# Moving two unit loads from ScalarE's to SyncE's queue, and turning the rows of three early jobs on VectorE instead of TensorE

## The chip, the cores and the metric

The kernel runs on one core of one Trainium2 chip. Its time is the time of one execution on the device, in microseconds (us); three runs were made of the kernel before, and one further execution was profiled. The profile names the engines PE (TensorE, matrix products and 128x128 transposes), PEld (TensorE's weight loads), DVE (VectorE), ACT (ScalarE), POOL (GpSimd) and SP (SyncE, which only issues DMAs). ACT, POOL and SP each have a queue of their own from which they issue DMAs; the profile writes ACTq, POOLq, SPq for it.

## The reference

The input is a sequence batch `x` of 4 x 3648 tokens of 256 channels, and a gate logit of the same shape. First comes a gated scan along each sequence, then a mixture of 16 experts in 4 groups (each token goes to one expert):

```python
f = lower_bound + (1 - lower_bound) * sigmoid(f_logit); i = 1 - f
for t in range(S): h = f[:, t] * h + i[:, t] * x[:, t]; y[:, t] = h      # 4 x 3648 x 256
x = y.reshape(14592, 256)
g_idx = argmax(x @ w_group); g_w = softmax weight of that group
e_idx = argmax(x[group g] @ w_expert[g]); e_w = softmax weight of that expert
out[token] = g_w * e_w * (relu(x[token] @ w1[g, e]) @ w2[g, e])          # 256 -> 1024 -> 256
```

## The kernel before, in words

The tokens are cut into 29 **units** of 512. A unit's input is one tile `zt` of 1 MB (gate logits and x, transposed: channels on partitions), loaded by `p1_load`. There are four `zt` buffers, so the load of unit u must wait until unit u-4 is through with its buffer. `ZX_SP = 9` decides which engine issues the load: units below 9 from SP's queue, the others from ACT's, where the issuing instruction stands in ACT's own order between its computations. Then ACT takes the tanh (L188) and an affine map (L198), DVE makes the gated input (L214, L234) and the scan `h` (L225), PE transposes `h` back to rows (L252), which ACT copies out as `rows` (L254, L256), and PE makes the router's scores (L266, L277; ACT copies them at L269 and L278 as `rs` and `Lg`). A chain of small DVE operations (L287 to L343, or to L382 in the first units) turns the scores of one or two units into a position `posi` for each token. POOL scatters the rows, 128 at a time, into lists by expert in a DRAM buffer `xs` (L347, an indirect DMA). A row of `xs` is 258 words: 256 channels, the token's number and its weight.

The experts' products are done in 32 **jobs** and a remainder. The first 16, the early jobs, one for each expert, run while the scan still goes on: `EARLY` gives for each a unit (the cut) and a number of 128-row tiles; the job takes so many rows of that expert's list as soon as the rows of all units before the cut are scattered. The early jobs 12 and 13 have 640 rows, 14 and 15 have 768. Then come 16 late jobs "B" with what is left in each list. A job loads its weights in 512 KB pieces `st` (L809), which ACT splits to a high part `wh` (L817) and DVE to a low part `wl` (L818); loads its rows (`job_rows`); brings them into the transposed form by `job_xt`; and multiplies in `m1_step` (L914 to L916, three products of high and low parts, then a relu `hh` on ACT at L919 and its low part `hl` on DVE at L920) and `m2_step` (L944). Loads, splits and transposes of a job are issued while the job before it multiplies; the rows of jobs 13 and 14 are asked for by `early_rows`, those of job 15 by `start_macro`, which runs after the last routing is issued.

In `job_rows` an early job loads each piece of up to 256 rows by one DMA (L791): partition p takes whole rows, 1032 bytes each. In `job_xt` PE then transposes each 128x128 block into a PSUM tile `ps_p` (L861), ACT casts it to `xh` (L870), DVE makes the low part `xl` (L871) and copies the tokens' numbers and weights to `meta` (L873). A job B does without PE: its rows come by four **quarter** loads (L767), each of which brings 64 of the 256 channels of all rows to 32 partitions in runs of 256 bytes, and DVE turns the 32x32 blocks in place (L848).

Each engine runs its instructions in an order that is fixed when the kernel is built: in the first part of the scan as the code issues them, later as a scheduler places them by its own estimate of when their operands come. DMAs of SP and ACT signal their ends on eight counters, DMAHW0 to DMAHW7, which the DMAs of both queues take in turn in the program's order; a DMA that takes a counter waits for the counter's last user to have landed. POOL's scatters use counters named DMASW. `early_loads` and `scatters` hold the row loads and the scatters already issued; `declare_no_dep` says of a pair that the one need not wait for the other.

Of the kernel before, what the change touches and what calls it, by code (L numbers as in the profile page):

```python
# [10 lines left out]
F32 = mybir.dt.float32  # L11
F16 = mybir.dt.float16
BF16 = mybir.dt.bfloat16
I32 = mybir.dt.int32
AF = mybir.ActivationFunctionType
ALU = mybir.AluOpType
AX = mybir.AxisListType.X

P = 128
# [18 lines left out]
X_BUFS = 4  # L38
AHEAD = 3
MT = -(-max(CAPS) // 128)  # L40
ZX_SP = 9


@with_exitstack
def gated_scan_moe(ctx: ExitStack, tc, zx, lower, wroute, wexp, out, S):
    nc = tc.nc
    sync = nc.sync
    ctx.enter_context(nc.allow_low_precision(reason="whole numbers small enough to be exact"))
    N, D = out.shape
    KD = D // P  # L50
# [9 lines left out]
    xs = nc.dram_tensor("xs", [LROWS, RW], I32).ap()  # L60
# [7 lines left out]
    mo = ctx.enter_context(tc.tile_pool(name="mo", bufs=2))  # L68
# [5 lines left out]
    def bank(tag):  # L74
        return ps.tile([P, UNIT], F32, name=f"ps_{tag}", tag=tag, bufs=PS_BUFS[tag])
# [79 lines left out]
    at = 0  # L155
# [7 lines left out]
    def p1_load(u):  # L163
# [13 lines left out]
        else:  # L177
            last_load[u] = (nc.sync if u < ZX_SP else nc.scalar).dma_start(out=zt[:, :, :, 0:w], in_=src[:, :, :, 0:w])
        units[u] = {"z": zt}
# [397 lines left out]
    def early_rows(u):  # L577
        asked.add(-u)
        for mac in macros:
            for j in mac:  # L580
                if j.kind == "A" and EARLY[j.idx][0] == u and j.idx < NE - 1:
                    job_rows(j)

    regs = {}
    early_loads = []
# [164 lines left out]
    def job_rows(j):  # L750
        e = job_e(j)
        queue = sync
        if j.kind == "A":
            pos = queue.value_load(j.pos[0:1, e:e + 1], min_val=e * LW + PRE - j.len, max_val=e * LW + PRE + N)
        elif j.kind == "B":
            pos = sync.value_load(regs["pordi"][0:1, j.idx:j.idx + 1], min_val=0,
                                  max_val=(NE - 1) * LW + PRE + N)
        else:
            pos = sync.value_load(regs["tabs"][0:1, 3 * j.idx + 1:3 * j.idx + 2], min_val=0, max_val=LIST)
        if j.kind != "A":  # L760
            job_mask(j)
        j.rows, j.meta = [], []
        if j.kind == "B":
            j.blocks = -(-j.len // 32)
            j.xb = p1.tile([P, 2, KD, UNIT], F32, name="zt", bufs=4).rearrange("p a b c -> p (a b c)")
            for q in range(P // 32):
                sync.dma_start(  # L767
                    out=j.xb.bitcast(I32)[32 * q:32 * q + 32, 0:j.blocks * KD * 32].rearrange("p (i c) -> p i c", c=KD * 32),
                    in_=xs[bass.ds(pos, j.blocks * 32), q * KD * 32:(q + 1) * KD * 32].rearrange("(i p) c -> p i c", p=32))
            j.info = mo.tile([P, MT + 1, 2], I32, name="info", bufs=6)  # L770
            full = [p for ps_ in j.parts for p in ps_ if p[2] == 1]
            nf, j.tails = len(full), [p for ps_ in j.parts for p in ps_ if p[2] > 1]
            sync.dma_start(out=j.info[:, 0:nf],
                           in_=xs[bass.ds(pos, nf * P), D:D + 2].rearrange("(t p) c -> p t c", p=P))
            for i, (b, _, g) in enumerate(j.tails):
                src = xs[bass.ds(pos + b, P // g), D:D + 2]
                for h in range(g):
                    sync.dma_start(out=j.info[h * (P // g):(h + 1) * (P // g), nf + i], in_=src)
            return
        for b, n in j.pieces:  # L780
            r = mo.tile([P, 2, RW], I32, name="xr", bufs=XR_BUFS)
            w = P if j.kind == "A" and j.tiles == 2 else n
            for q in range(0, n, w):
                at = pos + b + q
                if j.kind == "A" and b + q + w < j.len:

                    low = e * LW + PRE - (P if j.tiles == 2 else 2 * P)
                    above = at - low
                    at = ((above >= 0) * above + low).with_bounds(min_val=low, max_val=e * LW + PRE + N)
                m = w // P  # L790
                ld = queue.dma_start(out=r[:, q // P:q // P + m],  # L791
                                     in_=xs[bass.ds(at, w), :].rearrange("(p k) c -> p k c", k=m))
                if j.kind == "A":
                    early_loads.append(ld.ins)
                for u, sc in scatters:
                    if u >= EARLY[j.idx][0]:
                        tc.declare_no_dep(ld.ins, sc, reason="rows scattered behind a cut lie above it")
            j.rows.append(r)
# [21 lines left out]
    def job_xt(j, pi):  # L820
        b0, rows = j.pieces[pi]
        ch = max(i for i, (a, _) in enumerate(j.chunks) if a <= b0)
        c0 = b0 - j.chunks[ch][0]
        if j.raw:
            j.xh[ch] = mo.tile([P, 2 * P], F32, name="xh", bufs=X_BUFS)
            j.xl[ch] = mo.tile([P, 2 * P], F32, name="xl", bufs=X_BUFS)
        elif c0 == 0:
            j.xh[ch] = mo.tile([P, KD, 2 * P], F16, name="xh", bufs=X_BUFS)
            j.xl[ch] = mo.tile([P, KD, 2 * P], BF16, name="xl", bufs=X_BUFS)
        if j.kind == "B":  # L830
            if pi == 0:
                j.xt = p1.tile([P, 2, KD, UNIT], F32, name="zt", bufs=4).rearrange("p a b c -> p (a b c)")
                j.done = 0
                nf = j.tiles if not j.tails else j.tails[0][0] // P
                if nf:
                    nc.vector.copy_predicated(out=j.info[:, 0:nf, 0], mask=j.mask[:, 0:nf], data=nowhere[:, 0:nf])
                for i, (b, _, g) in enumerate(j.tails):
                    dest = mo.tile([P, 1], F32, name="dest", bufs=4)
                    nc.vector.tensor_scalar(out=dest, in0=rowmod[g], scalar1=regs["nclip"][:, j.idx:j.idx + 1],
                                            scalar2=-float(b), op0=ALU.subtract, op1=ALU.is_ge)  # L840
                    nc.vector.tensor_scalar(out=dest, in0=dest, scalar1=float(g * N), scalar2=part[g],
                                            op0=ALU.mult, op1=ALU.add)
                    col = j.info[:, nf + i, 0:1]
                    nc.vector.scalar_tensor_tensor(out=col, in0=col, scalar=float(g), in1=dest,
                                                   op0=ALU.mult, op1=ALU.add)
            upto = min(j.blocks, -(-(b0 + rows) // 32))
            xt = j.xt[:, 0:KD * j.blocks * 32].rearrange("p (k i r) -> p i k r", k=KD, r=32)
            nc.vector.transpose(out=xt[:, j.done:upto],  # L848
                                in_=j.xb[:, j.done * KD * 32:upto * KD * 32].rearrange("p (i c k) -> p i k c", k=KD, c=32))
            j.done = upto  # L850
            src = j.xt[:, 0:KD * j.blocks * 32].rearrange("p (k x) -> p k x", k=KD)[:, :, b0:b0 + rows]
            hi = j.xh[ch][:, :, c0:c0 + rows]
            nc.scalar.copy(hi, src)
            nc.vector.tensor_tensor(out=j.xl[ch][:, :, c0:c0 + rows], in0=src, in1=hi, op=ALU.subtract)
            return
        m = rows // P
        r = j.rows[pi]
        tp = bank("p")
        for k in range(KD):
            for t in range(m):  # L860
                nc.tensor.transpose(out=tp[:, (k * m + t) * P:(k * m + t + 1) * P],  # L861
                                    in_=r.bitcast(F32)[:, t, 0:D].rearrange("p (q k) -> p k q", k=KD)[:, k],
                                    identity=ident)
        tpv = tp[:, 0:KD * rows].rearrange("p (k w) -> p k w", k=KD)
        if j.raw:
            for k, t in enumerate((j.xh[ch], j.xl[ch])):
                nc.scalar.copy(t[:, 0:rows], tpv[:, k])
        else:
            hi = j.xh[ch][:, :, c0:c0 + rows]
            nc.scalar.copy(hi, tpv)  # L870
            nc.vector.tensor_tensor(out=j.xl[ch][:, :, c0:c0 + rows], in0=tpv, in1=hi, op=ALU.subtract)  # L871
        meta = mo.tile([P, 2, 2], I32, name="meta", bufs=16)
        tc.keep_in_program_order(nc.vector.tensor_copy(meta[:, 0:m], r[:, 0:m, D:D + 2]))  # L873
        if j.kind != "A":
            nc.vector.copy_predicated(out=meta[:, 0:m, 0], mask=j.mask[:, 0:m], data=nowhere[:, 0:m])
        j.meta.append(meta)
# [173 lines left out]
    at = 0  # L1050
# [67 lines left out]
    with tc.For_i(0, left, 1) as it:  # L1118
# [4 lines left out]
        j = make_job("X", 0)  # L1123
# [54 lines left out]
```

## Time and profile before

| what | us |
|---|---|
| three runs | 787.17, 792.07, 791.59 (median 791.59) |
| the profiled execution | 788.64 |
| its span from first to last instruction | 786.9 |
| PE busy | 717.1 (91% of the span) |
| DVE busy | 531.0 (67%) |
| ACT busy | 458.2 (58%) |
| POOL busy | 289.7 (37%) |

A row of a timeline has the start (us from the span's start), the busy time, the engine, the line, the operation with its tile names as out<-in, the shape and the count; the bracket holds the idle time ahead of it and what ended it. A row with SPq or ACTq is the issuing of a DMA. The windows give for each stretch the busy time of each engine, then the TensorE clock that was granted (1.00 is full speed), the mean busy share of the 16 DMA engines and what they moved.

### The profile page before, as it was taken

The numbers are of one execution on the slowest core, as the hardware profiler recorded it, in microseconds if no ns is written. First come the engines' busy times: TensorE is split into PE (matmuls) and PEld (weight loads), VectorE is DVE, ScalarE is ACT, GpSimd is POOL, SyncE is SP. The second block draws the span as 40 slices with busy tenths as digits, with TensorE's granted clock in tenths as the row PEclk, the third lists the DMA queues.
The fourth block names the chain that finished last, engine by engine and source line by source line (L and its number), as shares of the span: only waits on it lengthen the run. The fifth ranks groups of instructions, "written<-read, shape, count | busy, mean of one in ns | idle before, by whom it ended". The sixth has DMA issues, their size and how long they took to land.

```text
span 786.9 us, 20828 instructions
## 1 busy us (share of the span) xinstructions
PE 717.1 (91%) x8089; PEld 635.1 (81%) x8089; DVE 531.0 (67%) x1046; ACT 458.2 (58%) x822; POOL 289.7 (37%) x272
## 2 busy tenths in 40 slices
PE   2653896998999999999999999999999999999995
PEld 1432785777988888889988898999999999899995
DVE  6886699698999987585744646546554676556640
ACT  6674787676887956445444545444455465455541
POOL 3662328357456643642122212223232222222232
PEclk9855898999999999999999999999999999999998
DMA  7999898999988856377455443553554455555300
GB/s 271 345 347 298 267 291 262 318 284 276 331 320 287 286 169 196 121 248 183 131 132 108 130 105 112 140 124 111 139 161 111 147 165 169 166 141 175 98 30 24
DMA packets 93733, 151.75 MB, mean 193 GB/s; under 512 B 52481, under 2 KB 62623, under 8 KB 90304
## 3 DMA queue, kind: packets, MB, share of 16 engines
q1 hardware_dynamic: 78656, 99.90, 43.9%
q0 software_dynamic: 11424, 30.02, 10.7%
q10 hardware_dynamic: 3552, 20.48, 7.5%
q8 instruction: 64, 1.05, 0.6%
q14 instruction: 37, 0.30, 0.1%
HBM read 112.69 MB, written 38.19 MB: 192 GB/s over the span
## 4 chain that ended last, share of the span: by engine, by line
PE 63%; issue 11%; DVE 10%; DMA 9%; POOL 4%; ACT 2%; SPq 0%; POOLq 0%; DVEq 0%; ACTq 0%
PE ps_m L944 28%; PE ps_m L914 7%; PE ps_m L915 7%; PE ps_m L916 7%; DMA zt<-in_zx_dram 4%; DVE wl L818 3%; POOL out_dram L957 3%; PE ps_p L914 3%; PE ps_p L916 3%; PE ps_p L915 3%; DMA xr<-xs 2%; DVE h L225 2%; DVE hl L920 2%; PE ps_p L252 2%; DMA xs<-rows,posi 1%
## 5 line engine op out<-in xcount | busy, mean ns | idle before, releaser
L944 PE MATMUL ps_m<-wl,hh 128*128 128x256 bf16 (+4 forms) x1304 | 261.2, 251 | 1.7 <-issue 1.7
L944 PE MATMUL ps_m<-wh,hl 128*128 128x256 f16 (+4 forms) x1304 | 261.4, 251 | 0.0
L944 PE MATMUL ps_m<-wh,hh 128*128 128x256 f16 (+4 forms) x1304 | 261.0, 251 | 0.0
L944 PEld LDWEIGHTS <-hh 128*128 128x128 f16 (+2 forms) x2608 | 192.3, 99 | 25.0 <-issue 5.5
L914 PE MATMUL ps_m<-xh,wh 128*128 128x256 f16 (+11 forms) x766 | 191.7, 260 | 6.8 <-DVE hl L920 6.8
L915 PE MATMUL ps_m<-xl,wh 128*128 128x256 bf16 (+11 forms) x766 | 191.6, 260 | 0.3 <-DVE xl L871 0.3
L916 PE MATMUL ps_m<-xh,wl 128*128 128x256 f16 (+11 forms) x766 | 191.6, 259 | 0.0
L818 DVE TENSOR_TENSOR wl<-st,wh 128x1024 bf16<-128x1024 f32 x124 | 149.8, 1220 | 53.8 <-ACT wh L817 53.6
L347 POOL DMA_INDIRECT xs<-rows,posi x114 | 135.2, 1186 | 132.4 <-DVE rows L329 44.9
L957 POOL DMA_INDIRECT out_dram<-o,info x75 | 87.0, 1160 | 243.5 <-ACT o L956 226.7
L920 DVE SCALAR_TENSOR_TENSOR hl<-ps_m,hh 128x512 bf16<-128x512 f32 (+9 forms) x172 | 114.8, 670 | 78.5 <-ACT hh L919 78.0
L919 ACT ACTIVATE hh<-ps_m 128x512 f16<-128x512 f32 (+9 forms) x172 | 101.1, 588 | 66.3 <-PE ps_m L916 64.6
L817 ACT CAST wh<-st 128x1024 f16<-128x1024 f32 x124 | 128.1, 1047 | 16.6 <-PE ps_m L944 8.7
L915 PEld LDWEIGHTS <-wh 128*128 128x128 f16 x1072 | 105.0, 98 | 13.2 <-issue 5.7
L914 PEld LDWEIGHTS <-wh 128*128 128x128 f16 x1072 | 105.2, 98 | 10.0 <-issue 2.0
L916 PEld LDWEIGHTS <-wl 128*128 128x128 bf16 x1072 | 105.0, 98 | 8.0 <-issue 0.5
L944 PEld LDWEIGHTS <-hl 128*128 128x128 bf16 (+4 forms) x1304 | 102.9, 99 | 10.1 <-issue 0.2
L957 POOL DMA_INDIRECT out_dram<-o,meta x55 | 63.1, 1147 | 114.1 <-ACT o L956 103.3
L956 ACT ACTIVATE o<-ps_m,info 128x256 f32<-128x256 f32 (+4 forms) x75 | 33.0, 441 | 85.9 <-PE ps_m L944 78.4
L914 PE MATMUL ps_p<-xh,wh 128*128 128x256 f16 (+13 forms) x306 | 73.3, 252 | 0.0
L916 PE MATMUL ps_p<-xh,wl 128*128 128x256 f16 (+13 forms) x306 | 73.3, 252 | 0.0
L915 PE MATMUL ps_p<-xl,wh 128*128 128x256 bf16 (+13 forms) x306 | 73.3, 252 | 0.0
(165 smaller groups left out, 772.8 us busy)
## 6 DMA issues: line engine op xcount, KB each, us to landing
st<-in_wexp_dram SPq DMA_DIRECT2D x124, 512.0 KB, 6.6
zt<-in_zx_dram ACTq DMA_DIRECT2D x19, 1024.0 KB, 8.7
zt<-in_zx_dram SPq DMA_DIRECT2D x7, 1024.0 KB
xs<-blank SPq DMA_DIRECT2D x26, 258.0 KB, 4.3
xr<-xs SPq DMA_DIRECT2D x19, 258.0 KB, 5.2
xr<-xs SPq DMA_DIRECT2D x17, 129.0 KB, 2.4
xs<-rows,posi POOLq DMA_INDIRECT x114, 7.1
zt<-xs SPq DMA_DIRECT2D x8, 152.0 KB
```

The source lines that it names most:

```text
L225: nc.vector.tensor_tensor_scan(out=h[:, k, c0 - a:c1 - a], data0=ff[:, k, c0 - a:c1 - a], data1=uu[:, k, c0 - a:c1 - a], initial=init, op0 ...
L347: sc = nc.gpsimd.indirect_dma_start(out=xs_v[G["t0"] + t][:, :], out_offset=bass.IndirectOffsetOnAxis(ap=R["posi"][:, t:t + 1], axis=0), i ...
L817: nc.scalar.copy(j.wh[i], j.st[i])
L818: nc.vector.tensor_tensor(out=j.wl[i], in0=j.st[i], in1=j.wh[i], op=ALU.subtract)
L914: nc.tensor.matmul(po, w1_at(j.wh, k, c), xh[:, k], start=(k == 0), stop=False)
L915: nc.tensor.matmul(po, w1_at(j.wh, k, c), xl[:, k], start=False, stop=False)
L916: nc.tensor.matmul(po, w1_at(j.wl, k, c), xh[:, k], start=False, stop=(k == KD - 1))
L919: nc.scalar.activation(hi, pv, AF.Relu)
L920: nc.vector.scalar_tensor_tensor(out=j.hl[ch][:, cs[0]:cs[-1] + 1, 0:w], in0=pv, scalar=0.0, in1=hi, op0=ALU.max, op1=ALU.subtract)
L944: nc.tensor.matmul(pm[i * q:i * q + n, 0:dw], h[ch][:, c, ts], w2_at(w, c)[:, i * dw:(i + 1) * dw], start=(c == 0 and s == 0), stop=(c == ...
L956: nc.scalar.activation(o[s, 0:dw], pm[s, 0:dw], AF.Copy, scale=lt.bitcast(F32)[s, r, 1:2])
L957: nc.gpsimd.indirect_dma_start(out=out_v[out_n[0]].rearrange("n (g d) -> (n g) d", g=g), out_offset=bass.IndirectOffsetOnAxis(ap=lt[s, r, ...
```

## The change

`ZX_SP` becomes 11: the loads of units 9 and 10 (the tenth and eleventh) are issued by SP. And for the early jobs in `QUARTERS = (13, 14, 15)` each piece of rows is loaded as four quarters and a small DMA for numbers and weights; DVE turns the blocks from there into the PSUM tile, and PE's transposes and the copies of `meta` fall away.

```diff
-ZX_SP = 9
+QUARTERS = (13, 14, 15)
+ZX_SP = 11
...
                 m = w // P
+                if j.kind == "A" and e in QUARTERS:
+                    flat = r.rearrange("p a c -> p (a c)")
+                    for s in range(P // 32):
+                        ld = queue.dma_start(
+                            out=flat[32 * s:32 * s + 32, 0:KD * w].rearrange("p (i c) -> p i c", c=KD * 32),
+                            in_=xs[bass.ds(at, w), s * KD * 32:(s + 1) * KD * 32].rearrange("(i p) c -> p i c", p=32))
+                        early_loads.append(ld.ins)
+                    meta = mo.tile([P, 2, 2], I32, name="meta", bufs=16)
+                    ld = queue.dma_start(out=meta[:, 0:m],
+                                         in_=xs[bass.ds(at, w), D:D + 2].rearrange("(t p) c -> p t c", p=P))
+                    early_loads.append(ld.ins)
+                    j.meta.append(meta)
+                    continue
...
+        if j.kind == "A" and j.idx in QUARTERS:
+            tp = bank("p")
+            tpv = tp[:, 0:KD * rows].rearrange("p (k w) -> p k w", k=KD)
+            src = r.bitcast(F32).rearrange("p a c -> p (a c)")[:, 0:KD * rows]
+            nc.vector.transpose(out=tp[:, 0:KD * rows].rearrange("p (k i r) -> p i k r", k=KD, r=32),
+                                in_=src.rearrange("p (i c k) -> p i k c", k=KD, c=32))
+            hi = j.xh[ch][:, :, c0:c0 + rows]
+            nc.scalar.copy(hi, tpv)
+            nc.vector.tensor_tensor(out=j.xl[ch][:, :, c0:c0 + rows], in0=tpv, in1=hi, op=ALU.subtract)
+            return
         tp = bank("p")
```

The new path returns ahead of the loop that calls `declare_no_dep`, so these loads wait for every scatter that was issued before them. Each of the three jobs has three pieces: 256, 128, 256 rows in job 13 and 256 three times in 14 and 15. So 9 row loads become 36 quarter loads and 9 loads of `meta`; 10 + 12 + 12 = 34 transposes on PE become 9 on DVE; 9 copies of `meta` on DVE fall away.

Most lines behind the first insertion shift: L178 becomes L179, L188 L189, L278 L279, L559 L560, L791 L805, L809 L823, L818 L832, L871 L880 in the new path, L920 L944. New are L795 (a quarter load), L800 (the load of `meta`), L876 (the transpose on DVE) and L879 (the cast behind it).

**The order of ACT around the loads of units 11 and 12.** Here `rows` are the row copies, `rs` and `Lg` the router's copies, and L188 is the tanh of unit 9. Before:

```order
L254 COPY rows<-ps_p 128x2x256 [waits PE_49]
L178 DMA zt<-in_zx_dram 128x2048 [waits DMAHW2_49,DVE_49]
L269 COPY rs<-ps_p 128x128 [waits PE_49]
L178 DMA zt<-in_zx_dram 128x2048 [waits DMAHW5_49,DVE_49]
L278 COPY Lg<-ps_p 128x80 [waits PE_49]
L188 ACTIVATE zt<-zt 128x1024 [waits DMAHW3_49]
```

And in the changed kernel:

```order
L255 COPY rows<-ps_p 128x2x256 [waits PE_49]
L179 DMA zt<-in_zx_dram 128x2048 [waits DVE_49]
L270 COPY rs<-ps_p 128x128 [waits PE_49]
L179 DMA zt<-in_zx_dram 128x2048 [waits DMAHW3_49,DVE_49]
L279 COPY Lg<-ps_p 128x80 [waits PE_49]
L189 ACTIVATE zt<-zt 128x1024 [waits DMAHW2_49]
```

What moved: the second load, that of unit 12, waited for counter DMAHW5 and now waits for DMAHW3; its place among ACT's work is the same. The tanh behind it is in both that of unit 10, which waits for that unit's own load.

**The order of SP ahead of the first early rows**, which shows who uses these counters. `st` are weights, `blank` fills of the lists, `posA` the first early positions, `xr` the first early rows. Before:

```order
L809 DMA st<-in_wexp_dram 128x1024 [waits DMAHW7_49]
L559 DMA xs<-blank 128x258 [waits DMAHW0_49]
L559 DMA xs<-blank 128x258 [waits DMAHW1_49]
L559 DMA xs<-blank 256x1x258 [waits DMAHW2_49]
L754 TENSOR_LOAD posA [waits DVE_49]
L791 DMA xr<-xs 128x258 [waits DMASW5_49,DMASW4_49,DMASW6_49,DMASW3_49,DMASW7_49,DMASW2_49,DMAHW4_49,DMASW1_49,DMASW0_49]
L791 DMA xr<-xs 128x258 [waits DMAHW5_49]
```

And in the changed kernel:

```order
L823 DMA st<-in_wexp_dram 128x1024 [waits DMAHW6_49]
L179 DMA zt<-in_zx_dram 128x2048 [waits DMAHW7_49,DVE_49,Activation_49]
L560 DMA xs<-blank 128x258 [waits DMAHW0_49]
L560 DMA xs<-blank 128x258 [waits DMAHW1_49]
L179 DMA zt<-in_zx_dram 128x2048 [waits DMAHW2_49,DVE_49,Activation_49]
L560 DMA xs<-blank 256x1x258 [waits DMAHW3_49]
L755 TENSOR_LOAD posA [waits DVE_49]
```

What moved: the loads of units 9 and 10 stand ahead of the first and the third blank. Counter DMAHW5 is that of the second half of the first early rows (the last row of before); DMAHW3 is that of the last blank (the sixth row of the changed kernel).

**The order of DVE while job 12 multiplies and job 13 is prepared**, around the first transpose of job 14 in the changed kernel. `hl` is the low part of job 12's hidden layer, for which PE waits; `rest`, `key`, `h`, `rank` and so on belong to the one-time ordering of the lists. Before:

```order
L343 TENSOR_REDUCE posi<-sc 128x6
L612 TENSOR_TENSOR h<-key 128x256
L871 TENSOR_TENSOR xl<-ps_p,xh 128x512
L873 COPY meta<-xr 128x4
L319 TENSOR_REDUCE sm<-ex 128x30
L920 SCALAR_TENSOR_TENSOR hl<-ps_m_5124,hh 128x4x128
L321 SCALAR_TENSOR_TENSOR se<-sm,oh 128x24
```

And in the changed kernel:

```order
L880 TENSOR_TENSOR xl<-ps_p,xh 128x512
L344 TENSOR_REDUCE posi<-sc 128x6
L320 TENSOR_REDUCE sm<-ex 128x30
L944 SCALAR_TENSOR_TENSOR hl<-ps_m_5141,hh 128x4x128
L322 SCALAR_TENSOR_TENSOR se<-sm,oh 128x24
L601 SCALAR_TENSOR_TENSOR key<-rest,keyc 128x16
L876 STREAM_TRANSPOSE ps_p<-xr 128x8x2x32
L325 TENSOR_REDUCE s_5135<-se 128x6
```

What moved: the copy of `meta` is gone, and a transpose that waits for a quarter load stands between one `hl` and the next.

## Rows read from the trace of the kernel before

**Rows 1.** Page, part 1: busy us, share of the span, instructions.

```profile
PE 717.1 (91%) x8089; PEld 635.1 (81%) x8089; DVE 531.0 (67%) x1046; ACT 458.2 (58%) x822; POOL 289.7 (37%) x272
```

**Rows 2.** Windows by stage: start:end, length, the engines' busy time, clock, DMA share, GB/s.

```profile
60.00:85.00 25.00, 10.98 (x71) 7.85 (x72) 15.54 (x28) 11.60 (x25) 8.69 (x10) 0.57 0.92 309
...
120.00:190.00 70.00, 56.34 (x555) 47.22 (x553) 62.44 (x113) 51.03 (x95) 43.03 (x32) 0.95 0.89 281
190.00:290.00 100.00, 98.46 (x1029) 87.22 (x1027) 95.05 (x179) 78.22 (x146) 55.37 (x48) 1.00 0.86 289
290.00:390.00 100.00, 99.65 (x968) 89.70 (x966) 64.94 (x170) 50.77 (x89) 39.73 (x39) 1.00 0.58 175
```

**Rows 3.** ACT's timeline around the loads of units 11 and 12.

```profile
64.21 0.33 ACTq L178 DMA_DIRECT2D zt<-in_zx_dram  x1
65.16 0.27 ACT L269 COPY rs<-ps_p 128x128 f32<-128x128 f32 x1 [0.42 <-PE ps_p L266]
70.84 0.33 ACTq L178 DMA_DIRECT2D zt<-in_zx_dram  x1
71.22 0.23 ACT L278 COPY Lg<-ps_p 128x80 f32<-128x80 f32 x1 [5.79 <-DMA xr<-xs]
...
79.56 1.06 ACT L188 ACTIVATE zt<-zt 128x1024 f32<-128x1024 f32 x1 [4.57 <-DMA zt<-in_zx_dram]
```

**Rows 4.** Chain of waits of 59 to 92 us: start, length, what.

```profile
67.91 2.86 DMA xr<-xs
...
70.84 8.69 DMA zt<-in_zx_dram
...
81.14 1.13 PE ps_p L861 x4
```

**Rows 5.** The page's DMA issues: KB of one, median us from issue to landing.

```profile
xr<-xs SPq DMA_DIRECT2D x19, 258.0 KB, 5.2
```

**Rows 6.** Windows of 5 and 10 us, same columns as group 2.

```profile
75.00:80.00 5.00, 1.16 (x6) 0.75 (x4) 2.27 (x6) 0.44 (x1) 1.65 (x2) 0.50 1.00 414
...
330.00:340.00 10.00, 10.00 (x108) 9.15 (x105) 9.61 (x45) 3.69 (x9) 4.05 (x5) 1.00 0.42 134
...
360.00:370.00 10.00, 10.00 (x97) 8.99 (x95) 3.38 (x7) 3.67 (x7) 1.94 (x2) 1.00 0.94 159
```

**Rows 7.** Chain of waits of 300 to 395 us, job 14's first piece.

```profile
353.56 0.48 PE ps_p L861 x4
```

**Rows 8.** Instructions by line and form: count, busy us, mean ns, idle before.

```profile
L861 PE MATMUL ps_p<-ident,xr 128*128 128x128 f32 x110 | 19.3, 296 | 12.5 <-DMA xr<-xs 7.5 <-ACT rows L254 5.0
L871 DVE TENSOR_TENSOR xl<-ps_p,xh 128x512 bf16<-128x512 f32 x24 | 16.5, 685 | 8.9 <-ACT xh L870 8.8
...
L848 DVE STREAM_TRANSPOSE zt<-zt 128x512 f32<-128x512 f32 x18 | 12.5, 701 | 0.0
...
L873 DVE COPY meta<-xr 128x4 int32<-128x4 int32 x25 | 4.7, 187 | 0.0
```

**Rows 9.** DVE's timeline late in the scan.

```profile
334.37 0.68 DVE L920 SCALAR_TENSOR_TENSOR hl<-ps_m,hh 128x512 bf16<-128x512 f32 x1
...
340.89 0.68 DVE L920 SCALAR_TENSOR_TENSOR hl<-ps_m,hh 128x512 bf16<-128x512 f32 x1
...
379.96 0.70 DVE L848 STREAM_TRANSPOSE zt<-zt 128x512 f32<-128x512 f32 x1
```

**Rows 10.** SP's queue: row loads of jobs 14, 15, first job B.

```profile
329.95 1.69 SPq L791 DMA_DIRECT2D xr<-xs  x3
...
344.50 1.66 SPq L791 DMA_DIRECT2D xr<-xs  x3
...
359.04 3.94 SPq L767 DMA_DIRECT2D zt<-xs  x4
```

**Rows 11.** All 64 quarter loads of line 767.

```profile
DMA to landing us min/median/max: 1.7/3.5/7.7
```

**Rows 12.** POOL's timeline: the last scatter.

```profile
343.17 0.97 POOL L347 DMA_INDIRECT xs<-rows,posi  x1 [0.30 <-issue]
```

## The prediction

> **What bounds the kernel now.** I read the engines' totals first, then the windows by stage, then the chain of waits and the timelines of ACT, SP and DVE at the two places that the change touches.
>
> PE is busy for 717.1 us [rows 1], so a gain must take work from PE or shorten its idle time. The windows say where that is [rows 2]. From 60 to 85 us PE works 10.98 us of 25; from 120 to 190 it lacks 13.66 us; from 190 to 390 it is full (98.46 and 99.65 of 100). The reader is to see that in the first stretch no compute engine is full, while the DMA engines are at 0.92, and that from 190 to 290 DVE stands at 95.05.
>
> ACT's timeline tells why the first stretch is empty [rows 3]. At 65.16 ACT copies `rs`; then it is idle for 5.79 us, until the load of unit 12 has left its queue at 70.84, put down to "DMA xr<-xs". In the order this load waits for DMAHW5, the counter of the second half of the first early rows, and those wait for scatters. The router's copy `Lg` stands behind it (71.22), and DVE's routing, POOL's scatters and PE's transposes behind that. The chain of waits goes the same way [rows 4]: the rows' load 67.91 to 70.77, unit 12's load 70.84 to 79.53, ACT, PE at 81.14. ACT also waits 4.57 us ahead of unit 12's tanh at 79.56 [rows 3].
>
> **The change, part by part.**
>
> *Loads of units 9 and 10 to SP.* Two issues of 0.33 us each (the length of the one at 64.21 [rows 3]) leave ACT and enter SP. What counts is the counters: unit 12's load now waits for a blank, which SP issues ahead of the first early rows and which waits for no scatter. So it goes out right behind the copy at 65.16, which takes 0.27: at about 65.4 instead of 70.84, 5.4 us earlier. The first early rows stay behind their scatters; only loads of the scan come forward. On SP the two loads stand ahead of blanks; unit 10's waits for the buffer of unit 6, and the rows behind are not wanted before their scatters have landed, at 67.91 [rows 4], so I cost that at nothing. If that cover went, each us by which SP reaches the first rows later than 67.91 would cost one.
>
> The bounds of the gain: below nothing, if the transfers then meet in the stretch where the DMA engines are at 1.00 with 414 GB/s (75 to 80 us [rows 6]) and the rows of the early jobs land later; I allow 1.5 us for that, about the 8% that the engines lack to be full in 25 us, 2.0, less a part. Above, PE's transpose at 81.14 needs those rows, and 67.91 [rows 4] plus the median 5.2 us of such a load [rows 5] is 73.1: at most 8.0 us. I take **-4.5**: nearest to the 5.4 of the issue, less 0.9 because units 10, 11 and 12 now share the engines and the 8.69 us of unit 12's load [rows 4] grow. I take it to last to the end, since PE's later gaps (120 to 190) come from the same loop of scan, scatter and rows, which starts earlier as a whole. That is the weakest step.
>
> The Trainium skill, "Trainium Kernel Development and Optimization", Key Constraints, says that DMAs of the SP, ACT and POOL queues run on the same 16 engines, so issuing from several "only saves the sequencer's issue time". By that rule alone this part would be worth nothing and the sum 786.5; the trace's 5.79 us is a wait of the issuer for a completion, of which the rule does not speak.
>
> *Transposes of jobs 13 to 15.* 34 transposes leave PE. Four take 0.48 us in the chain [rows 7], 0.12 each (the mean of 296 ns by form [rows 8] counts overlapped time twice). PE is full there (99.65 of 100 [rows 2]), so 34 x 0.12 = **-4.1**. Bounds: 0 if PE waits for as much instead; -4.1 above.
>
> *On DVE.* Nine transposes come, eight of 128x512 and one of half that: the trace has them with an SBUF target at 701 ns [rows 8]. A PSUM target is not shown; `xl`, which reads PSUM, takes 685 ns for the same shape, so I take 0.70. That is at most 9 x 0.70 = 6.3 us, against nine copies at 0.187 = 1.7 us saved. DVE has 35 us to spare from 290 to 390 [rows 2], but not from 330 to 340: 9.61 of 10 [rows 6]. There job 14's first transpose now stands behind the `hl` of 334.37 and ahead of that of 340.89 [rows 9], with the ordering of the lists between; PE's products of job 12 use this `hl`. The copy that falls away gives 0.19 back, the transpose takes 0.70.
>
> *On the queues.* Each of the three jobs has 15 DMAs where it had 3. An issue costs 1.69/3 = 0.56 us at 329.95 and 3.94/4 = 0.99 at 359.04 [rows 10], so SP is held for 12 x 0.56 to 12 x 0.99, 7 to 12 us more per job. Job 14's first four quarters go out by 332.2 to 333.9; the median landing of a quarter is 3.5 us [rows 11], so they are there at 335.7 to 337.4, and the transpose is due near 335.1, behind the `hl` of 334.37 with its 0.68. That is a wait of 0.6 to 2.3 at a place with about as much loose work ahead of the next `hl`. Job 15's loads now wait for the last scatter, issued at 343.17 [rows 12], and so for its landing, a few us behind their 344.50 of now [rows 10]; they are turned from about 362 on, which covers this, and the weights behind them on SP. The first job B asks for its rows at 359.04 and turns them at 379.96 [rows 9, 10]: 21 us, less 7.7 for the slowest landing [rows 11], cover the delay on SP. If this cover went, DVE would stand still there too, with each next `hl` behind it. For DVE and queues together I take **+1.0** (0 to 6.3, the transposes' whole time; beyond that is a rival).
>
> The Trainium skill, "DMA: Bandwidth & Descriptors", Specifications, gives 512 bytes as the least transfer for line rate. The quarters' runs are 256 bytes. The trace agrees: while the first job B's quarters load, the engines are busy 0.94 for 159 GB/s, against 0.86 for 289 GB/s from 190 to 290 [rows 2, 6]. No term of the sum comes from this rule, but it is what stands behind the slower rival.
>
> **Sum:** -4.5 - 4.1 + 1.0 = -7.6 on the profiled execution's 788.64: 781.0. This execution lies 2.95 under the median of the three runs (791.59), between their ends 787.17 and 792.07, whose middle is 789.6. So I add 1.0: **782.0**.
>
> **The rivals.**
>
> *Early gain swallowed.* The part ahead of 85 us ends sooner, but from 85 to 290 the loop of loads, scan and scatters is held by DMA engines at 0.86 to 0.89 and by DVE at 95.05 of 100 [rows 2], and PE's gaps between 120 and 190 grow by what was won. For it: DVE's load there. Against it: DVE lacks 7.6 us of 70 from 120 to 190, and its own waits ahead of 85 go too. With half a us kept for the sum: -0.5 - 4.1 + 1.0 + 1.0 gives **786.0**.
>
> *More is won.* Unit 12's load comes so early that its 4.57 us wait goes as well, up to the bound of 8.0, and DVE's waits cost nothing new: 788.64 - 8.0 - 4.1 + 1.0 = **777.5**. Against it: DMA engines nearly full in that stretch.
>
> *Quarter loads late: slower.* DVE runs in order. When a quarter lands after its transpose's turn, the `hl` behind it and PE's `m2` products wait. Place: job 14's first piece near 335 and the pieces that follow, where the transposes stand well ahead of the place of PE's (353.56 [rows 7]); then job 15's and the first job B's rows, as 256-byte runs fill the engines. Price: up to the slowest landing, 7.7 us [rows 11], for each piece that is late. From 8.6 us of such waits on (4.5 + 4.1) the change is a loss; two late pieces of 7.7 on top of the sum, with the early gain swallowed, give 786.0 + 15.4 = **801.4**. Against it: of the nine pieces only job 14's are wanted within a few us of their issue.
>
> *It doesn't do what it says.* If unit 12's load were held by something else (its buffer, of unit 8), the early part would stay. That is the first rival's time.
>
> **Chances.** Forecast 0.50, with a range of its own of 779 to 785; early gain swallowed 0.28; more won 0.11; quarters late 0.11. About 1% is what a measurement of this kernel can tell from no change: below 783.7 it is faster by it, above 799.5 slower. The forecast's case lies four fifths below 783.7 (0.40), more won wholly (0.11), swallowed hardly (0.02): faster 0.53. Quarters late gives slower 0.09, the rest stays within 1%: 0.38. Range: 776 to 790, from below more won to beyond swallowed; it leaves out most of the slower rival and little at the lower end.
>
> **What would show it.** ACT's copy `Lg` at about 65.5 with no wait of 5.8 us, unit 12's tanh before 76, PE's first transposes of early rows at 76 to 77: step one. PE's idle time from 120 to 190 at 13.7 as before: it lasts; near 18: swallowed. No PE transposes from 320 on and PE still at 99% or more there: step two. DVE's transposes with waits of under 2 us put down to DMA: step three; waits of 5 and more with `hl` late: the slower rival. The prediction is wrong if the idle time of PE ahead of 85 us stays as it is, or if PE is idle for more than 3 us between 330 and 390.

## The result, and the profile after

| | before | changed |
|---|---|---|
| median of six runs, us | 789.45 (787.17 to 792.07) | 776.62 (775.32 to 780.02) |
| profiled execution, us | 788.64 | 776.59 |
| its span, us | 786.9 | 774.8 |

The ratio of the times is 0.9842, with a 95% interval of 0.9811 to 0.9873: about 12.5 us less. Forecast were 782.0 us and a range of 776 to 790; the time lies in it, 0.6 us above its lower end, but below the range of the forecast's own case (779 to 785). The windows by stage, with the columns of [rows 2]:

```profile
60.00:85.00 25.00, 19.09 (x114) 14.23 (x114) 17.99 (x30) 15.09 (x32) 10.99 (x11) 0.61 0.90 336
...
120.00:190.00 70.00, 59.66 (x574) 50.24 (x576) 59.27 (x110) 49.10 (x90) 39.70 (x34) 0.93 0.88 285
190.00:290.00 100.00, 98.45 (x1030) 87.34 (x1022) 93.97 (x177) 77.62 (x146) 56.84 (x47) 1.00 0.81 275
290.00:390.00 100.00, 99.24 (x967) 88.66 (x966) 66.67 (x157) 51.66 (x91) 37.45 (x36) 1.00 0.69 177
```

From 60 to 85 us PE works 19.09 us where it worked 10.98 [rows 2], with the DMA engines as busy as before (0.90 against 0.92), but moving more (336 against 309 GB/s). From 120 to 190 it lacks 10.3 us instead of 13.7: what was won ahead is not given back there. From 290 to 390 PE is at 99.24, a little less full than before. ACT's timeline around the loads of units 11 and 12, the part that answers [rows 3]:

```profile
64.59 0.27 ACT L270 COPY rs<-ps_p 128x128 f32<-128x128 f32 x1 [0.50 <-PE ps_p L267]
64.65 0.33 ACTq L179 DMA_DIRECT2D zt<-in_zx_dram  x1
65.42 0.23 ACT L279 COPY Lg<-ps_p 128x80 f32<-128x80 f32 x1 [0.56 <-PE ps_p L278]
...
69.34 1.06 ACT L189 ACTIVATE zt<-zt 128x1024 f32<-128x1024 f32 x1 [0.67 <-DMA zt<-in_zx_dram]
72.00 1.06 ACT L189 ACTIVATE zt<-zt 128x1024 f32<-128x1024 f32 x1 [1.61 <-DMA zt<-in_zx_dram]
```

Of the two tanhs shown, the first is unit 11's and the second unit 12's (the tanh in the two order listings of ACT is unit 10's). Unit 12's load leaves ACT's queue at 64.65, right beside the copy `rs`, and `Lg` follows at 65.42 with a wait of 0.56 us for PE, and none for a DMA. The tanh of unit 12 waits 1.61 us for its data instead of 4.57. The chain of waits of the same stretch:

```profile
63.81 0.84 DVE zt L235
64.65 7.33 DMA zt<-in_zx_dram
...
73.59 1.13 PE ps_p L885 x4
```

The load takes 7.33 us where it took 8.69 [rows 4], and PE's first transposes of early rows stand at 73.59 instead of 81.14: 7.55 us earlier, near the bound of 8.0. By this chain the load now starts when DVE is through with unit 8's buffer (L235, to 64.65), so with the counter out of the way it is the buffer that holds it.

For the second part, the instructions by line and form, with [rows 8] to compare:

```profile
L885 PE MATMUL ps_p<-ident,xr 128*128 128x128 f32 x76 | 13.8, 300 | 8.5 <-DMA xr<-xs 5.7 <-ACT rows L255 2.7
...
L876 DVE STREAM_TRANSPOSE ps_p<-xr 128x512 f32<-128x512 f32 x8 | 5.7, 716 | 0.4 <-DMA xr<-xs 0.4
```

There are 76 transposes on PE instead of 110, and DVE's, with a PSUM target, take 716 ns (701 with the SBUF target before). The landing of the 36 quarter loads, the queue that issues job 14's and 15's first quarters, and DVE at job 14's first transpose (`hl`, the transpose, the next `hl`):

```profile
DMA to landing us min/median/max: 2.1/2.2/2.8
```

```profile
323.13 2.49 SPq L795 DMA_DIRECT2D xr<-xs  x4
...
341.50 2.44 SPq L795 DMA_DIRECT2D xr<-xs  x4
```

```profile
326.60 0.68 DVE L944 SCALAR_TENSOR_TENSOR hl<-ps_m,hh 128x512 bf16<-128x512 f32 x1
...
327.84 0.73 DVE L876 STREAM_TRANSPOSE ps_p<-xr 128x512 f32<-128x512 f32 x1 [0.38 <-DMA xr<-xs]
...
333.31 0.67 DVE L944 SCALAR_TENSOR_TENSOR hl<-ps_m,hh 128x512 bf16<-128x512 f32 x1
```

A quarter lands 2.2 us after its issue. (The small loads of `meta` take longer, 6.3 us by the profile.) Job 14's first four go out from 323.13, and DVE waits 0.38 us for them; the next `hl` stands at 333.31, 6.7 us after the one ahead of it, much as before (6.5 [rows 9]). No other of the nine transposes waits for a DMA.

**Where the time comes off.** The relu `hh` of each step on ACT is in all these programs in the same number (239 records), so the difference of the starts shows where a kernel gains or loses. The table is worked out from ACT's timelines; the first column is the start in the kernel before, the others say by how much the same relu starts earlier (-) or later in a kernel (names as in the experiments below). The executions were taken on several chips, on which the median of the kernel before was 789.45 (beside the changed kernel), 791.27 (e1 to e4), 788.21 (e5) and 790.85 (e9). So a difference of 1 to 2 us between two columns tells little; a step within one column tells more:

| before, us | changed | e1 loads only | e2 quarters only | e3 wait back | e4 other counter | e5 changed again | e9 jobs 13, 15 |
|---|---|---|---|---|---|---|---|
| 96.50 | -6.70 | -7.99 | +1.23 | -0.68 | -5.49 | -6.92 | -6.48 |
| 149.08 | -6.46 | -8.11 | +1.11 | -0.40 | -2.62 | -6.74 | -5.78 |
| 309.51 | -6.44 | -8.01 | +1.16 | -1.18 | -2.13 | -6.91 | -5.71 |
| 338.69 | -7.63 | -8.02 | -0.03 | -1.19 | -2.14 | -8.10 | -6.90 |
| 369.55 | -8.59 | -8.09 | -0.73 | -1.18 | -2.13 | -8.99 | -7.14 |
| 389.33 | -10.03 | -8.09 | -2.17 | -1.19 | -2.13 | -10.43 | -8.58 |
| 665.15 | -9.95 | -8.09 | -2.08 | -1.18 | -2.13 | -10.26 | -8.57 |
| 696.79 | -11.81 | -8.87 | -3.94 | -1.40 | -2.56 | -11.87 | -10.43 |

The changed kernel gains 6.4 us ahead of 150, keeps them to 310, gains 1.2 at job 13, 1.0 at job 14 and 1.4 at job 15, and 1.9 in one place near 680.

### The profile page after: what moved, and what is told of

The parts are those of the page before. It is cut to its first block, busy times and chain, and to the rows that moved or that the text cites. A ratio compares the mean times of both kernels' runs of the same rounds, so it can differ in the third digit from the quotient of the medians.

```text
span 774.8 us, 20906 instructions
## 1 busy us (share of the span) xinstructions
PE 716.6 (92%) x8055; PEld 633.7 (82%) x8055; DVE 533.9 (69%) x1046; ACT 458.8 (59%) x822; POOL 286.6 (37%) x272
## 4 chain that ended last, share of the span: by engine, by line
PE 63%; DVE 11%; issue 10%; DMA 10%; POOL 4%; ACT 1%; SPq 0%; POOLq 0%; DVEq 0%; ACTq 0%
PE ps_m L968 29%; PE ps_m L938 7%; PE ps_m L939 7%; PE ps_m L940 7%; DMA xs<-rows,posi 4%; DMA zt<-in_zx_dram 3%; PE ps_p L938 3%; PE ps_p L940 3%; PE ps_p L939 3%; POOL out_dram L981 3%; DVE h L226 2%; DVE wl L832 2%; DMA xr<-xs 2%; PE ps_p L253 1%; DVE hl L944 1%
## 5 line engine op out<-in xcount | busy, mean ns | idle before, releaser
L832 DVE TENSOR_TENSOR wl<-st,wh 128x1024 bf16<-128x1024 f32 x124 | 149.6, 1218 | 55.2 <-ACT wh L831 54.0
L944 DVE SCALAR_TENSOR_TENSOR hl<-ps_m,hh 128x512 bf16<-128x512 f32 (+9 forms) x172 | 114.5, 668 | 74.5 <-ACT hh L943 73.7
L981 POOL DMA_INDIRECT out_dram<-o,meta x55 | 60.8, 1105 | 109.6 <-ACT o L980 98.6
```

Of the source, the lines that this page charges most:

```text
L832: nc.vector.tensor_tensor(out=j.wl[i], in0=j.st[i], in1=j.wh[i], op=ALU.subtract)
L944: nc.vector.scalar_tensor_tensor(out=j.hl[ch][:, cs[0]:cs[-1] + 1, 0:w], in0=pv, scalar=0.0, in1=hi, op0=ALU.max, op1=ALU.subtract)
L981: nc.gpsimd.indirect_dma_start(out=out_v[out_n[0]].rearrange("n (g d) -> (n g) d", g=g), out_offset=bass.IndirectOffsetOnAxis(ap=lt[s, r, ...
```

## The experiments

Two theories stood for the early part: that the gain is the **counter's** (unit 12's load no longer waits for the early rows), or that of **moving** units 9 and 10, which are then loaded earlier. For the second part: a transpose on PE is worth 0.12 us where PE is full and DVE keeps up, against a cost of the many small DMAs. Each ratio is to the kernel before on the same chip, with its 95% interval.

**e1, the loads alone.**

```diff
-QUARTERS = (13, 14, 15)
+QUARTERS = ()
```

> Only the loads of units 9 and 10 go to SP; jobs 13 to 15 keep their whole-row loads and PE's transposes. In the trace of the whole change the relus of the early jobs stand 6.4 us earlier than before from 150 to 310 us, ahead of every quarter load. If the early part is worth that alone: 6.4 us off the kernel before (789.45 to about 783.0), ratio 0.992, and PE's first transposes of early rows near 73.6 instead of 81.1. If part of it needed the quarters, or the two parts do not add up: under 4 us off.

Ratio 0.9895 (0.9866 to 0.9924); medians 782.43 and 791.27, so 8.8 us less, more than the 6.4 expected. PE's first transposes of early rows:

```profile
73.02 1.13 PE L885 MATMUL ps_p<-ident,xr 128*128 128x128 f32 x4 [2.54 <-ACT rows L255]
```

**e2, the quarters alone.**

```diff
-ZX_SP = 11
+ZX_SP = 9
```

> Only the quarter loads and DVE's transposes of jobs 13 to 15; units 9 and 10 are loaded from ACT's queue as before, with the stall at 65 us. By 34 transposes of 0.12 us less the 0.5 us that PE stands idle near 330 to 350: 3.6 us off (about 785.9), ratio 0.9955. If the quarters only gained beside the earlier start: no difference. The 1.85 us by which the whole change is shorter between 675 and 685 us should not be in either part if it is chance: then this kernel's relus end 3.6 us earlier than before, or 5.4 if the step comes with the quarters.

Ratio 0.9946 (0.9923 to 0.9969); 786.20 and 791.27. The stall is there as before, on ACT:

```profile
71.38 0.35 ACTq L179 DMA_DIRECT2D zt<-in_zx_dram  x1
71.77 0.23 ACT L279 COPY Lg<-ps_p 128x80 f32<-128x80 f32 x1 [6.10 <-DMA xr<-xs]
```

In the table e2 starts 1.2 us late, by chance or by its chip, since its program is that of before up to 290, and goes from +1.16 to -2.17 over jobs 13 to 15: 3.3 us. The product of the two ratios is 0.9842, the ratio of the whole: the parts add up.

**e3, the wait put back.** Units 9 and 10 stay on SP, no quarters.

```diff
+            if u == 12:
+                for i in range(2):
+                    nc.scalar.dma_start(out=spare[i:i + 1, :], in_=units[8]["h"][0:1, 0, 0:64])
             last_load[u] = (nc.sync if u < ZX_SP
```

> As the kernel with only the two loads moved, but two stores of 256 bytes to a spare buffer stand in ACT's queue ahead of the loads of units 11 and 12, so that unit 12's load again waits for the counter of the second half of the first early rows. If the gain is the counter's: the wait of about 5.8 us ahead of the copy Lg is back, PE's first transposes of early rows are at 79 to 81, and at most 1.5 us of the 6.4 are left (about 788 to 789.5). If it came from loading units 9 and 10 earlier: 6 us off stay (783).

Ratio 0.9981 (0.9956 to 1.0005); 788.89 and 791.27. ACT's timeline (the second store, unit 12's load, `Lg`) and PE's first early transposes:

```profile
64.76 0.25 ACTq L182 DMA_DIRECT2D spare<-h  x1
69.48 0.33 ACTq L183 DMA_DIRECT2D zt<-in_zx_dram  x1
69.85 0.23 ACT L283 COPY Lg<-ps_p 128x80 f32<-128x80 f32 x1 [4.83 <-DMA xr<-xs]
```

```profile
79.70 1.13 PE L889 MATMUL ps_p<-ident,xr 128*128 128x128 f32 x4 [4.92 <-ACT rows L259]
```

The wait is back with 4.83 us, the same releaser, and 6.8 of e1's 8.0 us (309.51 in the table) are gone, though the loads of units 9 and 10 leave SP within 1 us of e1's. By the medians of the runs 6.5 of e1's 8.8 us are gone.

**e4, the counter alone.** The kernel before, with fewer weight loads between the early rows and unit 12's load.

```diff
-        fetch_to(14)
+        fetch_to(9)
```

> The kernel before, with all its queues, but the weights of the second early job are fetched behind the first early rows' neighbours instead of ahead (9 weight pieces asked for at the start instead of 14); by this the load of unit 12 falls to the counter of a blank. No load is moved to SP. If the gain is the counter's: no wait ahead of the copy Lg, PE's first transposes of early rows at 73 to 76 us; the whole time is 4 to 6.5 us shorter unless the later weights make PE wait. If it came from loading units 9 and 10 on SP: no gain.

Ratio 0.9920 (0.9887 to 0.9952); 785.57 and 791.27.

```profile
66.46 0.33 ACTq L178 DMA_DIRECT2D zt<-in_zx_dram  x1
67.08 0.23 ACT L278 COPY Lg<-ps_p 128x80 f32<-128x80 f32 x1 [0.42 <-PE ps_p L277]
```

```profile
75.88 1.13 PE L861 MATMUL ps_p<-ident,xr 128*128 128x128 f32 x4 [2.99 <-ACT rows L254]
```

Nothing is moved to SP, and yet unit 12's load leaves at 66.46, `Lg` has no stall, and PE starts 5.3 us earlier than before. Of the 5.5 us at the first relu in the table 2.1 last; the rest goes between 96 and 127, where ACT waits once for 4.1 us for weights that now come later. (By the medians of the runs on one chip e4 gains 5.7 us; the table compares it with an execution on another.) Of the two theories the counter's holds; what moving the loads adds is small: 1.2 us by e3's column, 2.4 by its runs, whose interval reaches 1.

**e5, the whole change again**, beside e6 to e8.

> The whole change once more, on the chip of the three runs beside it. If the two parts add up: the product of their ratios, 0.9895 x 0.9946 = 0.984, so about 777 to 779 by the runs of before beside it. It also tells how far the early part differs from one profiled execution to the next: its relus from 150 to 310 us stood 6.4 us earlier than before, those of the loads alone 8.0, with the same program up to there.

Ratio 0.9852 (0.9822 to 0.9882); 774.99 and 788.21: close to the product again.

**e6, job 12 too**, `QUARTERS = (12, 13, 14, 15)`.

> The whole change, and job 12 by quarters too. Its 10 transposes leave PE where PE is full and DVE has room (DVE 5 to 6 of 10 us around 300). If a transpose on PE is worth 0.12 us wherever PE is full and DVE is not: 1.2 us less than the whole change, ratio 0.9985 of it. If the larger number of small DMAs begins to cost: no gain or a loss of 1 to 3.

Ratio 0.9891 (0.9864 to 0.9919); 779.00: it loses 4 us against e5, where the first expectation was a gain and the second a loss of at most 3. DVE (an `hl`, job 14's first transpose, the next `hl`, the second transpose, the `hl` after that), what PE waited for from 320 to 350 (in all, times, longest), and two windows:

```profile
323.20 0.68 DVE L944 SCALAR_TENSOR_TENSOR hl<-ps_m,hh 128x512 bf16<-128x512 f32 x1
...
327.17 0.73 DVE L876 STREAM_TRANSPOSE ps_p<-xr 128x512 f32<-128x512 f32 x1 [3.18 <-DMA xr<-xs]
...
328.98 0.68 DVE L944 SCALAR_TENSOR_TENSOR hl<-ps_m,hh 128x512 bf16<-128x512 f32 x1
...
334.09 0.71 DVE L876 STREAM_TRANSPOSE ps_p<-xr 128x512 f32<-128x512 f32 x1
...
335.11 0.67 DVE L944 SCALAR_TENSOR_TENSOR hl<-ps_m,hh 128x512 bf16<-128x512 f32 x1
```

```profile
PE ps_m L938 <- DVE hl L944: 3.4, 1, 3.4
```

```profile
330.00:335.00 5.00, 2.43 (x23) 2.04 (x21) 4.85 (x21) 1.70 (x3) 3.32 (x4) 1.00 0.50 107
335.00:340.00 5.00, 4.17 (x23) 3.03 (x23) 4.96 (x26) 2.79 (x4) 3.74 (x4) 0.66 0.67 169
```

In this kernel's order job 14's first transpose stands ahead of an `hl` that it stands behind in the changed kernel. It waits 3.18 us for the quarters, which go out only 1.1 us earlier than in the changed kernel (from 322.01), and all that stands behind it on DVE is late: this `hl`, the ordering of the lists and the second transpose. PE is not stopped by the `hl` at 328.98, but waits 3.4 us for the one at 335.11, and its granted clock is 0.66 over the next 5 us (the lower level, 1.2 GHz, for some two thirds of them), where it was 1.00 before. That is the slower rival of the prediction.

**e7, jobs 9 to 15**, `QUARTERS = (9, 10, 11, 12, 13, 14, 15)`.

> The whole change, and jobs 9 to 12 by quarters too: 10 + 3 x 8 = 34 more transposes leave PE. If PE is what bounds from 190 to 290 (98.45 of 100): 4.1 us less than the whole change. If DVE bounds there (93.97 of 100): six transposes of 0.70 us less six copies of 0.19 add 3.1 us to it, so 2.9 of the 4.1 turn to waits of PE for DVE and the time is that of jobs 12 to 15, or up to 2 us longer.

Ratio 0.9907 (0.9880 to 0.9935); 779.87. Window of the scan's last stretch, where jobs 9 to 11 are:

```profile
190.00:290.00 100.00, 98.17 (x1024) 86.27 (x1022) 99.15 (x182) 78.95 (x151) 56.03 (x48) 1.00 0.89 275
```

DVE goes from 93.97 to 99.15, PE stays at 98.17. At 309.51 its relus stand 9.12 us ahead of before, 2.7 better than the changed kernel, so part of the 4.1 is had; at job 14 the wait of e6 comes again (3.85 us), and 5 us are lost. Later its profiled execution loses another 4.2 us near 696, where PE pauses for 2.7 us without a reason in the profile and the granted clock is 0.78 and 0.88 in the two 5 us windows from 695 on.

**e8, unit 11 from SP too**, `ZX_SP = 12`.

> The whole change, and unit 11 is loaded from SP too; the load of unit 12 then waits for no DMA at all, that of unit 13 for the counter of the first of the second pair of early rows. By the counter theory unit 12's load goes out no earlier than it does (its buffer is free at 64.6), so the early part is the same within 1 us. If it is the moving to SP that gains: another 1 to 3 us.

Ratio 0.9914 (0.9883 to 0.9945); 780.84. ACT (unit 13's load and what stood behind it) and SP (units 10 and 11, the blank, the first early rows):

```profile
92.27 0.34 ACTq L179 DMA_DIRECT2D zt<-in_zx_dram  x1
92.64 0.59 ACT L255 COPY rows<-ps_p 128x512 f32<-128x512 f32 x1 [6.56 <-DMA st<-in_wexp_dram]
```

```profile
48.56 12.09 SPq L179 DMA_DIRECT2D zt<-in_zx_dram  x2
60.70 0.62 SPq L560 DMA_DIRECT2D xs<-blank  x1
70.69 3.01 SPq L805 DMA_DIRECT2D xr<-xs  x4
```

Moving one load more loses 5.9 us against e5; no change or a gain was expected. Unit 11's load waits on SP for its buffer until 60; the blank and the rows behind it go out late (70.69; 66.08 in the changed kernel), and on ACT the load of unit 13 now waits for a DMA of SP's queue: `rows` stands still for 6.56 us. The loss is at this place: the first relu of the early jobs is 7.5 us ahead of before (86.18 there), the one at 96.50 only 1.8. The stall has moved on by one unit.

**e9, jobs 13 and 15 only**, `QUARTERS = (13, 15)`; **e10**, `(12, 13, 15)`; **e11**, `(9, 10, 11, 12, 13, 15)`.

> The whole change, but job 14 as before: whole rows, 12 transposes on PE. In the trace of the whole change job 14's turning is worth its 12 x 0.12 = 1.4 us less about 0.5 us in which PE waits near 335. If so this kernel is 1.0 us slower than the whole change (ratio to before about 0.986). If the waits that job 14's quarters bring cost more than that: it is faster.

> Job 14 on PE, jobs 12, 13 and 15 by quarters. With jobs 12 to 15 DVE stood still for 3.2 us ahead of job 14's first transpose and PE for 3.4 behind it, and PE's clock fell to 0.66 in the 5 us after. If that wait is the loss: it is gone here, PE is at 99% or more from 290 to 390, job 12's 10 transposes give 1.2 us, and the time is within 0.5 us of the whole change's (ratio 0.984 to 0.985), some 4 us less than with jobs 12 to 15. If the number of small DMAs is what costs: 0.988 or more.

> Job 14 on PE, jobs 9 to 13 and 15 by quarters. With jobs 9 to 15 the relus around 310 us stood 2.7 us ahead of the whole change's, and 5 us were lost at job 14. If these are independent: 2.7 us less than the whole change up to 330, 1.0 us given back at job 14, so 1.5 to 2 us faster than the whole change (ratio to before near 0.982). If DVE, at 99 of 100 from 190 to 290, delays the scan instead: as the whole change or slower.

Ratios 0.9867 (0.9840 to 0.9894), 0.9839 (0.9806 to 0.9872) and 0.9857 (0.9824 to 0.9890); medians 779.61, 776.89 and 778.75, with 790.85 before. e10's window:

```profile
290.00:390.00 100.00, 99.81 (x973) 89.27 (x972) 65.80 (x157) 51.69 (x92) 39.18 (x36) 1.00 0.68 181
```

e9 comes out behind the changed kernel as expected (0.9867 against 0.9842 and 0.9852), though the intervals overlap; in the table job 14 gives it 0.2 us where it gave 1.0. In e10, without job 14's quarters, e6's loss is gone, and PE is full. So it was that wait. e10 has only as many quarter loads as the changed kernel (nine pieces of rows, e6 twelve), but e11 with fifteen doesn't have e6's loss either, so the number of small DMAs is not the cause. e10 is no faster than the changed kernel by what these runs can tell, and e11 is not either: its early part, where nothing is meant to differ from e10, came out 2.7 us later in the profiled execution (the first relu already), and it wins 3.4 us between 198 and 310, where e10 wins 1.2. No version beats the changed kernel clearly.

**e12, 34 small products ahead of PE's first work**, in the changed kernel.

```diff
+        warm = bank("p")
+        for i in range(34):
+            nc.tensor.transpose(out=warm[0:32, 0:P], in_=ident[:, 0:32], identity=ident)
```

> The whole change, with 34 small transposes (of the identity, used by nothing) ahead of PE's first work, where PE has nothing to do for 8 us; so PE's program has as many instructions as before at every later place. Near 680 us PE stands still for 0.9 to 1.7 us, waiting for nothing that the profile shows, in the four kernels without quarters (before, the loads alone, the wait put back, the other counter), and not at all in the six kernels with 22 to 34 or 56 fewer transposes that were looked at there. If this depends on how many instructions stand ahead on PE: the pause of 0.9 to 1.7 us is back near 672, between the relus that stand at 675 and 687 us in the kernel before, and the time is 1 to 2 us longer than the whole change's. If it comes with the quarters themselves (their DMAs, DVE's or ACT's order): no pause, the whole change's time.

Ratio 0.9839 (0.9795 to 0.9883); 824.73 and 838.49, on a chip on which both kernels take 6% longer. What PE's weight loads waited for without a reason in the profile (in all, times, longest):

```profile
PEld L968 <- issue: 6.7, 20, 0.9
```

With pauses in 20 places on that chip, the one asked for can't be told apart. The ratio is that of the whole change, but its interval of 0.9% covers the 1 to 2 us in question. Inconclusive.

## Why the prediction was right, and where its sizes were off

The mechanism was right in both parts; the sum was 4.5 us short. In the profiled executions the change is 12.05 us (788.64 to 776.59) where 7.6 was summed: 6.4 for 4.5 ahead of 310, 3.6 for 3.1 in jobs 13 to 15, and 1.9 near 680 for which the sum had no term. That the time still lies in the stated range is owed to its width: the time is nearer to the rival "more is won" (777.5, chance 0.11) than to the forecast.

- **The stall and its cause** (right). The counter that unit 12's load waits for is what changed; e3 and e4 show it from both sides. A rival that the prediction lacks, PE's clock ahead of 85 us, doesn't fit: from 30 to 60 us the granted clock is 0.57 before, 0.55 in e1, which has the whole gain, and 1.00 in e2, which has none.
- **The early term, -4.5** (mechanism right, size too small). It measures -6.4 in the profiled execution, -8.0 in e1's. With no edit to the early part it differs by up to 4 us from one execution to the next: over the eight executions with it (changed, e1, e5, e6, e7, e9, e10, e11: 6.46, 8.11, 6.74, 5.77, 6.13, 5.78, 6.99 and 3.92 earlier at 149.08) against the two without (0 and +1.11) it is 6.8 on average. Two steps are mis-sized. The load leaves 6.2 us earlier, not 5.4, since it goes out beside the copy `rs`, and that copy is 0.6 us earlier. And "less 0.9 because units 10, 11 and 12 now share the engines and the 8.69 us of unit 12's load grow" has the wrong sign: the load became 1.4 us shorter (7.33). Together these are the 7.55 us by which PE's first transposes come forward. The wait ahead of unit 12's tanh shrank from 4.57 to 1.61, because the data come 7.55 us earlier and ACT's work ahead of it only 4.6. The bound of 8.0 was a little too low: e1's transposes, at 73.02, are 8.1 us ahead, and there the first early rows go out earlier too (from 66.1 instead of 67.3), which the bound had left where they were.
- **That it lasts** (right; called the weakest step). The shift is -6.70 at 96 us and -6.44 at 309. The rival of the swallowed gain falls: neither DVE nor the DMA engines took the gain back. DVE is at 93.97 of 100 from 190 to 290, and e7 wins time there with DVE at 99.15.
- **-4.1 on PE and +1.0 on DVE and the queues** (right: -3.1 forecast, -3.6 measured in the changed kernel, -3.3 in e2). Jobs 13 and 15 give 1.2 and 1.4, 10 and 12 times 0.12; job 14 gives 1.0 of its 1.4. The wait there was 0.38 us where 0.6 to 2.3 was forecast: a quarter lands in 2.2 us, not 3.5. PE waits 0.8 us for `hl` between 290 and 390, 0.3 before.
- **The slower rival** (right in kind, not in this kernel). e6 and e7 have it at the very place, with waits of 3.18 and 3.85 us and with the price that the rival lacked: the fall of PE's clock behind the pause. The changed kernel, in whose order the transpose stands behind an `hl` more, waits 0.38 us there. The order, which the prediction had read, kept it from that price; e6 shows that one more job by quarters is enough to change the order.
- **Issuing from several engines "only saves the sequencer's issue time"** (the Trainium skill, "Trainium Kernel Development and Optimization", Key Constraints). Taken alone it gave 786.5, where 776.62 was measured. For the move by itself the rule agrees with e3 (loads moved, wait back: 0.9981, with an interval that reaches 1). What it doesn't speak of is the wait behind which a load stands, and that changes with the queue: e1's 0.9895 and e8's loss.
- **Not forecast:** the 1.9 us near 680. In the kernel before, PE stands still there after a run of 158 small products, waiting for nothing that the profile shows; e1 has it at 674.57 (chain of waits, start, length, what):

```profile
677.95 4.71 PE ps_m L944 x158
682.66 1.68 issue
```

```profile
674.57 0.91 issue
```

e3 and e4 have it too (1.47 and 1.25 us), the changed kernel, e2 and e5 to e11 don't have it at that place. So it goes with the quarters, which take instructions from PE ahead of that place; e7, with the fewest, has its pause of 2.7 at 695.67. That it hangs on where PE's instructions lie is argued and not shown, and e12 could not decide it: the cause stays open. With it e2's quarters are worth 4.2 us at the end of the span (782.7 against 786.9), or 5.1 from its late start, instead of 3.3.

## What to carry to other kernels

When an engine's copy or activation is idle "for a DMA" that it doesn't read, look at the DMA that the same engine issues just ahead of it: it may be waiting for the completion of an unrelated transfer, on the counter that both use, and everything in that queue waits with it. Which transfer that is can change with every DMA added or moved, so after any such edit read the order with its waits again (e8 moved the stall from unit 12 to unit 13). Work moved to an engine that runs in order cost next to nothing here where its operands were there at its turn (0.38 us late in the changed kernel); where they were 3 us late (e6, e7), the full engine behind it lost that time and, for some microseconds, its clock.

## What the runs showed of the hardware

Blocks of 64 KB in 256-byte runs landed in 2.2 us (2.1 to 2.8), whole rows of 258 KB in 4.9 in the same kernel. Four such blocks make a piece of rows and take 2.5 us to issue, so the last is there about 4.7 us after the first issue: the short runs did not make the rows later, although the engines' share from 290 to 390 rose from 0.58 to 0.69 for much the same 175 and 177 GB/s. That agrees with what the Trainium skill says of short transfers ("DMA: Bandwidth & Descriptors", Specifications: 512 bytes for line rate), and here it cost no time that these runs show. Still shorter runs were slow to land: a `meta` load, 2 KB in runs of 8 bytes, took 6.3 us. A pause of 3.4 us in a stretch with PE otherwise full was followed by a granted clock of 0.66 over 5 us (e6).
